# Transformer block: row maxima taken by key blocks ahead of the steps, projections dealt out beside them

## The chip, the cores and the metric

The kernel runs on one core of a Trainium2 chip. The metric is device time in microseconds of one execution, the median of the runs shown; smaller is better. The core's engines are TensorE (PE, with its weight loads PEld), VectorE (DVE), ScalarE (ACT), GpSimd (POOL) and SyncE (SP), which here only issues DMAs. Each engine works through its own queue in order and waits on semaphores for the others.

## The reference, cut to what matters

```python
# x: 1 x 2048 x 576, 32 heads of 18, feed-forward width 4608
qkv = (layernorm(x) @ wqkv)                       # -> q, k, v per head
scores = q @ k.T * 18 ** -0.5
o = softmax(scores) @ v
h = x + o @ wo
g, u = layernorm(h) @ w_gate, layernorm(h) @ w_up
out = h + (gelu_tanh(g) * u) @ w_down
```

Inputs and outputs are float32. The softmax subtracts each row's true maximum, so every score is computed twice: once for the maximum, once for the exponential.

## The kernel before, in words

**Numbers.** Operands are split into two half-precision parts (hi and lo), and a product is a sum of three matmuls, hi·hi, lo·hi, hi·lo. `products` (L264) lists the 14 pairs of one 576-long contraction, `accumulate` (L273) issues them into one PSUM bank.

**Start.** The 2048 rows are cut into 4 blocks of 512. A block is normalized (`ln_stats`, `rstd_of`, `ln_rows`, L372 to L381: DVE, with copies on ACT and differences on POOL), and DMA transposes (`turn`, L230) bring it into XT. The 1152 columns of Q and K are 9 tiles of 128 (tiles 0 to 4 hold Q, 4 to 8 hold K): `qk_tile` (L324) makes one tile for one block, 14 matmuls of 512 columns, ACT takes hi out of the bank, DVE takes lo, and SP stores both to DRAM (L333, L334). `v_rows` (L337) makes V for 128 rows, two times 14 matmuls of 288 columns. An order written out by hand (L404 to L477) interleaves all this; `manual_schedule` keeps PE, ACT, DVE and POOL in program order until L865, and SP in it for L404 to L474. Loads of weights and x are on SP's queue, some placed late in this order. The projections that are left form the generator `other_products` (L785): V of blocks 1 to 3, then Q and K tiles 1, 6, 2, 7, 3, 8 of blocks 1 to 3.

**Attention.** Four heads form a group, 8 groups. For a group, `load_stacks` (L504) reads Q and K from DRAM into a stack set (18 hi, hi, lo rows of each head, two heads to a 128-row tile, so a contraction of 54); half of these loads are on SP, half on POOL. There are two sets, used in turn. A block n (0 to 31) is a group with 512 queries; it has 16 steps, one for each 128 keys.

- *Maxima.* A unit (`max_unit`, L519) is 128 queries against 512 keys for four heads. It has two halves; a half is two matmuls into two banks (L529) and two DVE reductions along them (L532). 16 units make a block. Within a block the query tile t is the slow index, the key block kc the fast one. After 16 units `max_finish` (L540) sends the maxima as two more rows into the Q stacks, so that the score matmul subtracts them. `maxima` (L643) runs through all 512 units, one half per `take`.
- *Scores.* `scores_pair` (L569): two matmuls (L576) into a pair of banks, then one Exp over 1024 columns on ACT (L578) into one of NPE = 4 buffers. Two pairs a step.
- *Weighing.* `weigh` (L580): four matmuls in float32 (L582, eight in the trace) that add the weighted values to `acc`.
- *Block end.* `out_block` (L590) divides by the sums (POOL, and DVE for the last four blocks) and writes into XT.

PSUM has eight banks: two pairs for the scores, one for `acc`, and the three others in a ring for the maxima. Before the steps all four singles are that ring.

**Order of the steps.** After 14 pieces of `other_products`, 24 units (`AHEAD`, L641) run with three pieces after each (L803). Then come 512 steps (L808 to L842). A step issues: half a unit, both score pairs, two pieces of what is left to fill, half a unit, and `weigh` of the step before. The maxima so end 24 steps before the scores. During the last blocks the fill is `wo_block` (L675): the output projection of 128 rows and 288 columns a piece, residual addition on DVE (L684), layer norm, split and transposes, through a single buffer `y`. `prepare_wo` and `split_gate_up` make the next weights ready as `side`.

**Feed-forward.** 9 chunks of 512 columns, gate, up and down (L745 to L782), bound by PE.

## Time and profile before

| what | us |
|---|---|
| three timed runs | 2893.16, 2901.07, 2901.41 |
| median | 2901.07 |
| span of the profiled execution | 2899.4 |
| PE busy in it | 2752.8 |
| DVE busy | 1942.0 |
| ACT busy | 1432.5 |
| POOL busy | 321.8 |

The page gives the span from the first to the last instruction; what lies around it isn't shown by it. Times inside the trace are counted from the span's start. PE counts as busy from the start of a matmul to its modelled end, also where several overlap. In a row of the timeline stand the start, the length, the engine, the line, the operation with what it writes and reads, and the number of instructions merged into it; in square brackets the idle time before it and what ended it. In a row of the chain stand start, length, engine and line. In a row of groups stand after the bar the busy time, the mean length of one in ns, and the idle time before.

### The profile page before, as it was taken

Reading aid. Unit: us, or ns where it says so; the run is one execution under the profiler, and the core shown is the slowest. Engines: PE = TensorE matmul, PEld = TensorE weight load, DVE = VectorE, ACT = ScalarE, POOL = GpSimd, SP = SyncE. Lnnn points to the kernel's source line nnn. Section 1 sums busy time; section 2 is a strip of 40 time slices with the busy share of each in tenths; the row PEclk is TensorE's granted clock in tenths of the full one; section 3 lists DMA queues with packets and bytes.
Section 4 is the critical chain, followed back from the end, with each engine's and each line's share of the span. In section 5 each row is a group of like instructions: output and inputs, shape, how many; then the busy total and the mean of one; then the engine's idle time right before and its main releaser. Section 6 shows DMA issues by size and latency. Waiting matters only on the chain.

```text
span 2899.4 us, 42932 instructions
## 1 busy us (share of the span) xinstructions
PE 2752.8 (95%) x17178; PEld 1152.0 (40%) x17178; DVE 1942.0 (67%) x3485; ACT 1432.5 (49%) x1626; POOL 321.8 (11%) x484
## 2 busy tenths in 40 slices
PE   7999999999999999999887999999999999999999
PEld 3542222222222222222223555555555555555555
DVE  6369999999999999999864725252525252524222
ACT  4217888888888888888563312121212121212111
POOL 2102421222212221212100000000000000000000
PEclk9999999999999999999998999999999999999999
DMA  8211110101001010101113301010101010100001
GB/s 216 67 58 39 40 35 14 38 14 32 14 18 34 14 38 12 35 14 50 40 45 93 96 1 53 1 53 1 53 1 53 1 53 1 53 1 1 1 17 50
DMA packets 109404, 105.08 MB, mean 36 GB/s; under 512 B 61780, under 2 KB 79828, under 8 KB 109204
## 3 DMA queue, kind: packets, MB, share of 16 engines
q1 hardware_dynamic: 102964, 89.98, 11.0%
q0 software_dynamic: 5712, 11.19, 1.4%
q8 instruction: 134, 2.20, 0.3%
q10 hardware_dynamic: 528, 1.18, 0.1%
q14 instruction: 66, 0.54, 0.1%
HBM read 72.09 MB, written 14.42 MB: 30 GB/s over the span
## 4 chain that ended last, share of the span: by engine, by line
PE 50%; DVE 43%; ACT 3%; DMA 2%; issue 1%; SPq 1%; POOL 0%; POOLq 0%; DVEq 0%; ACTq 0%
DVE mx L532 40%; PE pair L278 32%; PE bank L278 16%; PE bank L582 1%; PE bank L529 1%; ACT W L252 1%; ACT V L252 1%; DMA X<-V 0%; ACT V L739 0%; PE pair L576 0%; ACT W L739 0%; DMA X<-A 0%; ACT WK L578 0%; DMA A<-qk_hi 0%; DVE st L185 0%
## 5 line engine op out<-in xcount | busy, mean ns | idle before, releaser
L532 DVE TENSOR_REDUCE mx<-bank 128x1 f32<-128x512 f32 x2048 | 1265.0, 683 | 28.6 <-PE bank L529 28.5
L578 ACT ACTIVATE WK<-pair,p_ex_sc 128x1024 f32<-128x1024 f32 x1024 | 1084.6, 1113 | 235.8 <-PE pair L576 234.8
L582 PE MATMUL bank<-WK,V 128*32 128x512 f32 x4096 | 549.7, 608 | 0.1
L278 PE MATMUL pair<-X,V 128*128 128x512 f16 x2240 | 491.4, 381 | 8.8 <-ACT ga L756 8.6
L278 PE MATMUL pair<-X,W 128*128 128x512 f16 x2044 | 447.4, 379 | 1.5 <-ACT ga L756 1.5
L759 DVE SCALAR_TENSOR_TENSOR ga<-pair,p_hsc,ga 128x512 f32<-128x512 f32 x144 | 107.8, 749 | 506.3 <-PE pair L278 500.6
L278 PEld LDWEIGHTS <-WK 128*128 128x128 f16 x3456 | 338.1, 98 | 93.8 <-issue 0.5
L756 ACT ACTIVATE ga<-pair,p_gsc 128x512 f32<-128x512 f32 x144 | 98.8, 686 | 483.4 <-PE pair L278 483.4
L278 PEld LDWEIGHTS <-W 128*128 128x128 f16 x2296 | 223.7, 98 | 284.5 <-issue 13.6
L529 PE MATMUL bank<-W 54*128 54x512 f16 x1024 | 291.5, 382 | 43.1 <-DVE mx L532 14.1
L278 PEld LDWEIGHTS <-V 128*128 128x128 f16 x2240 | 219.4, 98 | 271.4 <-issue 14.8
L529 PE MATMUL bank<-A 54*128 54x512 f16 x1024 | 279.4, 382 | 36.0 <-DVE mx L532 6.1
L760 ACT CAST WK<-ga 128x512 f16<-128x512 f32 x144 | 88.9, 618 | 436.9 <-DVE ga L759 436.9
L779 DVE SCALAR_TENSOR_TENSOR nat<-bank,p_dsc,nat 128x288 f32<-128x288 f32 x288 | 147.7, 516 | 196.8 <-PE bank L278 196.8
L582 PEld LDWEIGHTS bank<-WK,V 128*32 128x32 f32 x4096 | 81.3, 108 | 434.4 <-issue 406.3
L278 PE MATMUL bank<-V,WK 128*128 128x288 f16 x1920 | 239.5, 286 | 0.2 <-DVE nat L779 0.2
L278 PE MATMUL bank<-W,WK 128*128 128x288 f16 x1536 | 191.4, 286 | 0.0
L576 PE MATMUL pair<-W 56*128 56x512 f16 x1024 | 159.3, 379 | 6.0 <-ACT WK L578 5.4
L576 PE MATMUL pair<-A 56*128 56x512 f16 x1024 | 156.5, 377 | 1.6 <-ACT WK L578 0.8
L761 DVE TENSOR_TENSOR WK<-ga,WK 128x512 f16<-128x512 f32 x144 | 99.3, 690 | 78.1 <-ACT WK L760 77.9
L605 POOL TENSOR_TENSOR rp<-rc,minus_one 128x16 f32<-128x16 f32 x28 | 81.9, 2924 | 616.3 <-DMA rc<-nat 616.3
L529 PEld LDWEIGHTS <-W 54*128 54x128 f16 x1024 | 59.3, 93 | 222.0 <-issue 220.0
(170 smaller groups left out, 1276.9 us busy)
## 6 DMA issues: line engine op xcount, KB each, us to landing
V<-in_B_w_down_dram SPq DMA_DIRECT2D x8, 1152.0 KB
nat<-rc SPq DMA_DIRECT2D x32, 256.0 KB
A<-in_B_w_gate_dram SPq DMA_DIRECT2D x8, 1024.0 KB
A<-in_B_w_up_dram SPq DMA_DIRECT2D x8, 1024.0 KB
qk_hi<-qk SPq DMA_DIRECT2D x36, 128.0 KB
qk_lo<-qk SPq DMA_DIRECT2D x36, 128.0 KB
A<-in_A_x_dram SPq DMA_DIRECT2D x32, 144.0 KB
out_dram<-nat SPq DMA_DIRECT2D x16, 288.0 KB
```

What stands on the lines that cost most here:

```text
L278: nc.tensor.matmul(dst, a, b, start=(i == 0), stop=(i == len(pairs) - 1))
L529: nc.tensor.matmul(pms[j][:, :TB], Q[r, q0 : q0 + P], K[r, kc * TB : (kc + 1) * TB], start=True, stop=True)
L532: nc.vector.tensor_reduce(mx[:, t, 2 * pr + j, kc : kc + 1], pms[j][:, :TB], axis=AX.X, op=ALU.max)
L576: nc.tensor.matmul(pS[:, j, :TB], K[r, kt * P : (kt + 1) * P], Q[r, qc * TB : (qc + 1) * TB], start=True, stop=True)
L578: nc.scalar.activation(pes[(2 * kt + pr) % NPE], pS[:, :, :TB], AF.Exp, scale=ex_sc)
L582: nc.tensor.matmul(acc[32 * hh : 32 * hh + 32, :TB], Vg[n // NB][:, kt * G4 + hh * VC : kt * G4 + hh * VC + 32], pes[(2 * kt + hh // 2) % ...
L605: nc.gpsimd.tensor_tensor(rc, den, minus_one.to_broadcast([P, R]), op=ALU.pow)
L756: nc.scalar.activation(ga, pg[:, :TB], AF.Gelu_apprx_tanh, scale=gsc)
L759: nc.vector.scalar_tensor_tensor(ga, pu[:, :TB], hsc, ga, op0=ALU.mult, op1=ALU.mult)
L760: nc.scalar.copy(hh[:, f], ga)
L761: nc.vector.tensor_sub(hl[:, f], ga, hh[:, f])
L779: nc.vector.scalar_tensor_tensor(nat[:, t, ws], pt[:, :HALF], dsc, nat[:, t, ws], op0=ALU.mult, op1=ALU.add)
```

## The change

The maxima begin earlier, all projections move ahead of the first step, and the maxima that are left are spread evenly over the steps.

1. **Start.** The loads of the K weights and of x for blocks 1 to 3 go on POOL's queue at the very start. Of the hand-written order remain tiles 0, 1, 4, 5, 2, 3, 6, 7 of block 0 and tiles 4, 5 of block 1, with the norms of all four blocks among them. For the first group, the rows of Q and K go from the tile in SBUF straight into the stacks (`stack_rows`, for tiles 0, 4 and 5) and not by way of DRAM. For most tiles the difference lo moves from DVE to a second ACT copy and a POOL subtraction (`pool=True`). V's memsets come later, weights lie in another order in W.
2. **Maxima ahead.** A unit's fast index is now the query tile, the slow one the key block, so that the first units need only key block 0. `accumulate` yields after every five matmuls and says how many columns it issued; `feed` deals out 2300 columns after every half unit until the projections are used up. The units that have run by then (`lead`) are ahead of the steps.
3. **Steps.** One score pair of the next step is issued between the halves. A plan (`wanted`) says how many units should have run after step k; the step takes 0 to 3 halves. NPE is 5. One piece of `fill` a step instead of two.
4. **Output projection.** `y` is a ring of four buffers (two for the last block), and POOL makes the split for blocks 0 to 2.

```diff
+    def feed(it, columns, owed):
+        owed[0] += columns
+        while owed[0] > 0:
+            c = next(it, None)
+            if c is None:
+                return False
+            owed[0] -= c
+        return True
...
+    load_w(wf[1], wqkv[:, D:QK], nc.gpsimd)
+    for b in range(1, NB):
+        load_x(b, nc.gpsimd)
...
+    def stack_rows(j, b, hl):
+        sl = slice(b * TB, (b + 1) * TB)
+        of_k = j > 0
+        first = j * P - (D if of_k else 0)
+        for h in range(4):
+            lo_r, hi_r = max(h * DH, first), min((h + 1) * DH, first + P)
+            if lo_r >= hi_r:
+                continue
+            T = sets[0][h // 2][of_k]
+            o = 64 * (h % 2) + lo_r - h * DH
+            n = hi_r - lo_r
+            src = slice(lo_r - first, hi_r - first)
+            for i, k in enumerate((0, 1, 0) if of_k else (0, 0, 1)):
+                nc.sync.dma_start(T[o + i * DH : o + i * DH + n, sl], hl[src, k])
...
-        nc.vector.scalar_tensor_tensor(lo, bank[:, :TB], 2.0 ** -16, hi,
-                                       op0=ALU.mult, op1=ALU.subtract)
+        if pool:
+            f = next(late_parts)
+            nc.scalar.activation(f, bank[:, :TB], AF.Copy, scale=2.0 ** -16)
+            nc.gpsimd.tensor_sub(lo, f, hi)
+        else:
+            nc.vector.scalar_tensor_tensor(lo, bank[:, :TB], 2.0 ** -16, hi,
+                                           op0=ALU.mult, op1=ALU.subtract)
+        if stack:
+            stack_rows(j, b, hl)
...
+    qk_tiles(0, 4, stack=True)
+    ln_rows(4, 2, **on_pool)
+    qk_tiles(0, 5, stack=True)
+    ln_rows(6, 2, **on_pool)
+    cut(s, 6, 7, 8)
+    qk_tiles(0, 2, 3, pool=True)
+    ln_block(2)
+    ln_rows(8, 4, **on_pool)
+    qk_tiles(0, 6, pool=True)
+    ln_stats(12, 2)
+    qk_tiles(1, 4, stack=True)
+    ln_stats(14, 2)
+    rstd_of(12, TPB, root=True)
+    qk_tiles(1, 5, stack=True)
+    ln_rows(12, 4, **on_pool)
+    qk_tiles(0, 7, pool=True)
...
-        t, kc = divmod(u, NB)
+        kc, t = divmod(u, TPB)
...
-    NPE = 4
+    NPE = 5
...
+    def other_products():
+        for b in (2, 3):
+            for j in (4, 5):
+                yield from qk_tile(j, b, stack=True)
+        yield from qk_tile(0, 1, pool=True, stack=True)
+        for t in range(NT):
+            if t == NT // 2:
+                yield from qk_tile(0, 2, pool=True, stack=True)
+            yield from v_rows(t)
+        yield from qk_tile(0, 3, pool=True, stack=True)
+        for b in range(1, NB):
+            yield from qk_tile(1, b, pool=True)
+        init_set(sets[1])
+        load_stacks(1)
+        yield from qk_tile(8, 0, pool=True)
+        for j in (6, 2, 7, 3, 8):
+            for b in range(1, NB):
+                yield from qk_tile(j, b, pool=True)
+
+    SLACK = 4600
...
+    while more:
+        for _ in range(2):
+            half_units(1)
+            more = feed(fill, SLACK // 2, owed)
...
+    END = NSTEP - NT - 4
+    def wanted(k):
+        loaded = 2 + max(0, (k - 8) // (NB * NT))
+        return min(lead + (NU - lead) * (k + 1) / END, 64 * loaded, NU)
...
+    scores_pair(0, 0, 0)
+    for k in range(NSTEP):
+        n, kt = step(k)
...
+        due = min(3, int(2 * (wanted(k) - state["units"])))
+        scores_pair(n, kt, 1)
+        if due > 1:
+            half_units(1)
+        if k + 1 < NSTEP:
+            scores_pair(*step(k + 1), 0)
+        if k:
+            pn, pk = step(k - 1)
+            weigh(pn, pk, acc)
...
+        take(fill)
+        take(side, 2 if g == NG - 1 else 1)
+        half_units(due - 1 if due > 1 else due)
...
+            y = next(y_pool if b < NB - 1 else y_last)
```

More of the change, by code (lines that the diff above doesn't have):

```diff
@@ new lines, in tile_block @@
+    for t in (2, 3):
+        normed(nat[:, t], nat[:, t], t)
+    take(n0, 3)
+    split_rows(parts[2], nat[:, 2], **on_pool)
+    s = [result(n0), None]
+    idle_products(18)
+    split_rows(parts[3], nat[:, 3])
+    turn(parts[2], 2)
+    turn(parts[3], 3)
+    cut(s, 0, 1, 2, 3, 4)
+    load_w(wf[2], wqkv[:, QK:], nc.sync)
+    take(n1, NK + 1)
+    qk_tiles(0, 0, stack=True)
+    s = [None, result(n1)]
+    cut(s, 4, 5)
+    qk_tiles(0, 1)
+    ln_block(1)
+    qk_tiles(0, 4, stack=True)
@@ L843, in tile_block @@
+        if n and kt in ((3, 6) if late else (2, 4)):
+            take(ob)
+        if late and kt == 9:
+            run(fill)
+            fill = wo_block(qc - 1)
+        if g and g + 1 < NG and kt == 2 and qc == 0:
+            load_stacks(g + 1)
+        if n == NS - NB and kt == 2:
+            load_gate_up(0, nc.gpsimd)
+        if n == NS - 2 and kt == NT * 3 // 4:
+            side = keep(split_gate_up(0, nc.vector.tensor_scalar_mul))
     run(side)
     run(fill)
-    weigh(*prev)
-    ob = out_block(prev[0], prev[2])
+    weigh(*step(NSTEP - 1), acc)
```

260 lines of the change are left out of this document (96 added, 164 removed).

## The prediction, made before the changed kernel had run

> **What bounds the kernel now.** I read the page, then the windows, the groups of the middle stage, one step of the timeline, and the chain of waits. One chip run lies behind all rows: a span of 2899.4 us, 1.7 us under the median of the timed runs (2901.07), and I add that back at the end.
>
> ```profile
> span 2899.4 us, 42932 instructions
> L532 DVE TENSOR_REDUCE mx<-bank x2048: 626/680/693, 120.8 to 1465.1; 128x1 f32<-128x512 f32 x187
> L578 ACT ACTIVATE WK<-pair,p_ex_sc x1024: 1106/1114/1174, 226.4 to 1560.4; 128x1024 f32<-128x1024 f32 x171
> 120.80:226.40 105.60, 102.05 (x592) 49.81 (x593) 72.21 (x117) 19.62 (x46) 0.69 (x3) 0.98 0.16 50
> 226.40:1382.00 1155.60, 1088.29 (x7419) 247.72 (x7418) 1151.00 (x1897) 996.85 (x967) 271.53 (x391) 1.00 0.10 27
> 1382.00:1562.50 180.50, 147.00 (x1016) 54.06 (x1012) 126.34 (x277) 101.78 (x99) 18.81 (x27) 0.91 0.23 56
> L532 DVE TENSOR_REDUCE mx<-bank 128x1 f32<-128x512 f32 x1601 | 988.6, 683 | 0.0
> L578 ACT ACTIVATE WK<-pair,p_ex_sc 128x1024 f32<-128x1024 f32 x800 | 848.4, 1112 | 136.4 <-PE pair L576 135.6
> ```
>
> The first maximum is taken at 120.8, the first Exp at 226.4. In the window rows the columns are length, PE, weight loads, DVE, ACT, POOL. From 120.8 to 226.4 PE is full (102 of 105.6) and DVE is not. From 226.4 to 1382.0 stand 464 of the 512 steps (blocks 0 to 28). The last two rows are groups of 388.2 to 1382.0, 400 steps, so 2.485 us a step: DVE looks full with reductions (988.6 of 993.8), ACT idles 136 us. A step has two half units of maxima (two matmuls and two reductions each), two score pairs with an Exp each, one weigh. So far this says that DVE is the bound. Inside one step it reads otherwise:
>
> ```profile
> 807.46 0.39 PE L529 MATMUL bank<-A 54*128 54x512 f16 x2
> 807.68 0.60 PE L576 MATMUL pair<-W 56*128 56x512 f16 x4
> 808.12 0.88 PE L529 MATMUL bank<-A 54*128 54x512 f16 x2
> 808.63 0.37 PE L529 MATMUL bank<-A 54*128 54x512 f16 x1
> 808.93 1.07 PE L582 MATMUL bank<-WK,V 128*32 128x512 f32 x8
> 809.93 0.39 PE L529 MATMUL bank<-A 54*128 54x512 f16 x2
> 807.88 0.69 DVE L532 TENSOR_REDUCE mx<-bank 128x1 f32<-128x512 f32 x1
> 808.49 1.28 DVE L532 TENSOR_REDUCE mx<-bank 128x1 f32<-128x512 f32 x2
> 810.35 0.69 DVE L532 TENSOR_REDUCE mx<-bank 128x1 f32<-128x512 f32 x1
> 811.09 0.37 PE L529 MATMUL bank<-A 54*128 54x512 f16 x1
> ```
>
> These are PE's issue order (maxima, two score pairs, maxima, weigh, maxima) and single reductions. The second matmul of the second half unit stands alone at 808.63, because its bank, of three, comes free only when the reduction begun at 807.88 ends. From there a **loop** runs: to weigh 0.30 (808.93), weigh to the next maxima 1.00 (809.93), matmul start to reduction start 0.42 (810.35), the reduction 0.69, release 0.05, and at 811.09 the same matmul waits again. That is 2.46, the step. Two reductions in a row take 1.28, so they can start 0.60 apart; four need 2.40 and DVE has a little slack that its busy time hides. PE, the three banks and DVE's latency bound the step together, and PE's order in the queue sets what lies in the loop. The score pairs lie outside it, between the halves.
>
> Without maxima a step is bound by ACT: six Exps in 6.14 are 1.00 apart, so 2.01 a step. PE goes from a score pair to weigh in 0.33.
>
> ```profile
> 1467.99 0.39 PE L576 MATMUL pair<-W 56*128 56x512 f16 x2 [0.54 <-ACT WK L578]
> 1468.32 1.07 PE L582 MATMUL bank<-WK,V 128*32 128x512 f32 x8
> 1492.28 6.14 ACT L578 ACTIVATE WK<-pair,p_ex_sc 128x1024 f32<-128x1024 f32 x6 [2.95 <-PE pair L576]
> ```
>
> **The change, 1: the start.** All projections now end before the first step, so 46 more units run ahead, and the first maximum comes earlier.
>
> ```profile
> 0.00:20.00 20.00, 7.84 (x30) 3.17 (x31) 14.45 (x44) 11.24 (x23) 6.79 (x24) 1.00 0.86 228
> 5.20 6.47 DMA WK<-in_A_wqkv_dram
> 16.48 3.35 DMA X<-A
> 19.96 7.71 PE bank L278 x35
> 15.11 2.74 SPq L231 DMA_TRANSPOSE X<-A  x2
> 1533.28 0.70 SPq L635 DMA_DIRECT2D X<-nat  x1
> 1534.02 0.70 SPq L634 DMA_DIRECT2D X<-nat  x1
> L333 SPq DMA_DIRECT2D qk_hi<-qk x36: 319/320/665, 23.8 to 225.1; - x36
> ```
>
> The last two numbers of the window row are the DMA share, 0.86, and 228 GB/s. The loads of the first weights, landed at 11.7, let projections begin at 19.96. POOL's queue now starts 4.9 MB (the K weights, the x of blocks 1 to 3) beside the first 2.6 MB. At 228/0.86 = 265 GB/s shared evenly, the first 2.6 MB end near 19 instead of 11.7: +7, between 0 (no sharing) and +18 (all of the 4.9 MB first). I take 7, so projections begin near 27. The rule that speaks against this move stands in the Trainium skill, DMA: Bandwidth & Descriptors, Issuing engines are not separate DMA queues: transfers started by different engines end up on the same 16 DMA engines and interleave. By it the even share holds; without it this term would be 0. No row here shows the two queues loading large blocks at once.
>
> Then SP's queue sets the pace. In its fixed order it now issues the stack rows from SBUF to SBUF: 12 for tiles 0 and 4, 3 for tile 5. The nearest row with the same shape (18 rows of 1 KB) is issued every 0.74 (1533.28 to 1534.02). Ahead of block 1's last transpose stand 27 x 0.74 = 20.0, eight stores of 0.32 = 2.6, four transposes of 1.37 = 5.5, in all 28 from 31.5 (tile 0 done), and 3.4 to land: 63. PE then owes tiles (4, block 1), (5, block 1) and 7, 9 us, and DVE closes block 3's norm: first maximum near **76**, against 120.8 (60, if a stack row costs SP only the 0.32 of a store and the weights come on time; 90, if they come last). Behind it SP still has 4 + 4 transposes and the stacks of blocks 1 to 3; key block 2 lands near 101 where the maxima want it at 96, key block 3 some 2.5 late too: **8** us (0 to 15). Hi and lo conversions, now by ACT and POOL for most tiles, hide under PE, which needs 3 us a tile; the V memsets hide on POOL.
>
> ```profile
> 148.53 2.68 PE pair L278 x21
> 191.80 4.64 PE pair L278 x21
> 1416.71 0.32 PE bank L529 x2
> 1413.17 3.54 PE bank L278 x28
> 1418.78 3.54 PE bank L278 x28
> ```
>
> From the first maximum to the first step PE does 26 tiles of 14 matmuls at 4.64/21 = 0.221, 80.4; 448 V matmuls at 2.68/21 = 0.128, 57.2; and, one half unit per 2300 columns, 315392/2300 + a few = 140 halves at 0.32 between wide matmuls, 44.8. Sum 182; DVE needs 140 x 1.20 and some 8 for splits, 176, and hides beside it. So the lead is 70 units, and steps start at 76 + 182 + 8 = **266** (245 to 285): **+40** on 226.4.
>
> **2: the steps.** PE's order is now: score pair 1, maxima, score pair 0 of the next step, weigh, maxima. The three banks stay. With two halves the lonely second matmul is that of the first half, and between it and the next maxima stand a score pair (0.22, from 807.46 to 807.68) and weigh: 0.22 + 0.33 + 1.00 + 0.42 + 0.69 + 0.05 = **2.70** instead of 2.46. Queued behind the waiting matmul are that score pair, weigh and so the next maxima; DVE waits for these, 0.3 a step. The second score pair hides in the reduction. A step with one half has no matmul that waits: two pairs, 0.33 and weigh, **1.76** from maxima to maxima; ACT's 2.01 is met on the average with its longer neighbours, thanks to the fifth buffer.
>
> Up to step 464 the plan asks for 0.898 units a step, 833 halves. It is capped at 128 units until step 72: eight steps with none (2.01), then about twelve with three (2.70 + 1.20). The other 444 have 798 halves: 354 with two, 90 with one. 354 x 2.70 + 90 x 1.76 + 8 x 2.01 + 12 x 3.90 = 955.8 + 158.4 + 16.1 + 46.8 = 1177. The reduction at a block's end fits into DVE's idle time.
>
> ```profile
> 403.37 0.50 POOL L517 DMA_DIRECT2D A<-qk_hi  x1 [0.55 <-DMA A<-qk_lo]
> A<-qk_hi POOLq DMA_DIRECT2D x32, 72.0 KB, 6.7
> ```
>
> Step 72 wants the stacks of the next heads 16 us after block 4 begins. Now their last is issued 15 us after it (403.4 against 388.2) and lands 6.7 later, behind POOL's reciprocal work: 5 us of wait, and 1 at step 136. So 1183, 2.55 a step, against 1155.6: **+27** (an average of 2.40 a step would give -42, 2.65 gives +74).
>
> **3: the end.** Blocks 29 to 31 now take one piece of the output projection a step instead of two, POOL splits three row blocks, and four y buffers replace one. Before, such a step lasted 5.6 (1413.17 to 1418.78), and 12 us went into two waits:
>
> ```profile
> PE bank L131 <- DVE am_gu L127: 7.6, 1, 7.6
> DVE WK L214 <- POOL V L228: 4.5, 2, 2.3
> ```
>
> PE stood before the exponents' transposes, DVE before POOL had read y (us in total, times, longest). After, a step with one product is 2.70 + 1.8 + about 0.5 for DVE's addition in its line, 5.0; without maxima 3.4. Block 29: 10 x 2.5 + 6 x 5.0 = 55; block 30: 56; block 31: 48 with 4 of waiting for the last rows; 3.4 left over: 162 against 180.5: **-18** (-30 to 0). What follows 1562.5 is unchanged.
>
> **The sum:** +40 + 27 - 18 = +49 on the span, and 2901 + 49 = **2950**.
>
> **The rivals.**
> - *DVE is the bound (faster).* Its occupancy speaks for it, the 0.60 spacing against it. A half would cost 2.485/2 = 1.24 wherever it stands: 833 x 1.24 + 16 of idle + 6 = 1055, -100 instead of +27: 2901 - 78 = 2823. It decides if the loop breaks, which needs a fourth bank or a shorter queue. The Trainium skill, Perfetto Trace Analysis, Identifying the Most-Contended Engine, takes the occupancy of the vector engine as a fair measure of its distance from the roofline; by that rule this rival would be the forecast, while the row at 808.63 speaks against it.
> - *The order costs nothing.* Steps with two halves stay at 2.485, those with one fall to ACT's 2.01: 354 x 2.485 + 90 x 2.01 + 16 + 12 x 3.7 + 6 = 1127, -29: 2901 + 40 - 29 - 18 = 2894, no change. For it: the loop's extra 0.24 is a sum of gaps, each taken from another order.
> - *A step with one half lasts as long as ACT, 2.01, and the first maxima wait for SP until 86 (slower still):* 90 x 0.25 + 10 = +32: 2982.
> - That the maxima don't run 70 ahead is ruled out by the count of columns above.
>
> **How the numbers follow.** Forecast 0.52, DVE bound 0.15, order free 0.17, slower still 0.16. The predicted time is the forecast's. 0.3% (9 us) is about what a measurement of this kernel tells from no change. Faster by more: 0.15, and 0.08 of the second rival and of the forecast's low edge: 0.23. Within: 0.11. Slower: 0.66. The likeliest case has 2905 to 2995 for itself: its terms' ends lie some 20, 55 and 15 away, the root of their squares is 60, and three quarters of it are taken; the range reaches down over the second rival, 2865, and up to 2995, and leaves out DVE bound and the worst of the last.
>
> **What would show it.** Right: the first reduction near 76 and the first Exp near 266; steps of about 2.70 and 1.76 in the middle with DVE idle some 0.3 before a reduction that waits for PE; a stretch of 2.0 then 3.9 near step 64. Wrong: an average step under 2.4, single second matmuls that don't wait, or a first Exp before 240.

## The result, and the profile after

The changed kernel takes **2995.21 us** (median of 4 runs, 2993.31 to 3000.92) against 2901.24 of the kernel before (4 runs beside it): ratio **1.034**, 95% interval 1.0322 to 1.0357. The direction was forecast; the size was about half of what came, and 2995.21 lies just above the range's top of 2995. The profiled execution of the changed kernel is the longest of its four, 3000.92 (5.7 above the median), and its span is 2999.1; so some 6 of the 51 in the last row below belong to that execution.

Cut at the same marks as in the prediction (step 464 is the first of block 29; "last Exp" is the start of the last one), the spans are:

| stretch, us | before | forecast | after | missed by |
|---|---|---|---|---|
| start to the first reduction of the maxima | 120.8 | 76 | 83.8 | +8 |
| first reduction to first Exp | 105.6 | 190 | 202.8 | +13 |
| steps 0 to 463 | 1155.6 | 1183 | 1186.8 | +4 |
| step 464 to the last Exp | 178.3 | 160 | 172.2 | +12 |
| last Exp to the end | 1339.0 | 1339 | 1353.4 | +14 |
| span | 2899.4 | 2948 | 2999.1 | +51 |

So the middle, on which most of the prediction's argument stood, came out within 4, and the two ends were sized wrong, all in one direction.

From the page of the changed kernel, the groups of the reductions and of the Exps (line numbers have moved: reduction L542, its matmuls L539, score matmuls L586, Exp L588, weigh L592, accumulate L277), and below them the reductions in the page of the kernel before:

```profile
span 2999.1 us, 43163 instructions
...
L542 DVE TENSOR_REDUCE mx<-bank 128x1 f32<-128x512 f32 x2048 | 1277.6, 683 | 161.6 <-PE bank L539 159.1
L588 ACT ACTIVATE WK<-pair,p_ex_sc 128x1024 f32<-128x1024 f32 x1024 | 1105.2, 1116 | 242.3 <-PE pair L586 231.7
```

```profile
L532 DVE TENSOR_REDUCE mx<-bank 128x1 f32<-128x512 f32 x2048 | 1265.0, 683 | 28.6 <-PE bank L529 28.5
```

DVE now idles 161.6 ahead of its reductions, where it was 28.6, and PE ends that idling. The windows of the changed kernel for the three middle stretches follow, the last one up to the end of the last Exp. The columns are as in the prediction; the third number from the right is PE's granted clock as a share of full speed.

```profile
83.80:286.60 202.80, 193.67 (x1084) 81.47 (x1084) 183.09 (x299) 52.17 (x123) 42.34 (x69) 0.99 0.24 69
286.60:1473.40 1186.80, 1047.70 (x7220) 236.08 (x7223) 1041.23 (x1700) 1013.51 (x956) 261.05 (x367) 0.99 0.09 23
1473.40:1647.10 173.70, 143.15 (x990) 49.30 (x983) 122.91 (x247) 104.35 (x100) 28.64 (x36) 0.94 0.24 55
```

In the steps no engine is full any more: DVE is busy for 1041 of 1187, where it was 1151 of 1156. One step with two halves, from the timeline of the changed kernel:

```profile
1007.96 0.37 PE L539 MATMUL bank<-A 54*128 54x512 f16 x1 [0.34 <-DVE mx L542]
1007.96 0.59 PE L586 MATMUL pair<-A 56*128 56x512 f16 x2
1008.48 1.07 PE L592 MATMUL bank<-WK,V 128*32 128x512 f32 x8
1009.48 0.39 PE L539 MATMUL bank<-A 54*128 54x512 f16 x2
1009.70 0.38 PE L586 MATMUL pair<-A 56*128 56x512 f16 x2
1009.92 0.38 PE L539 MATMUL bank<-A 54*128 54x512 f16 x1
1010.65 0.37 PE L539 MATMUL bank<-A 54*128 54x512 f16 x1 [0.34 <-DVE mx L542]
1009.90 2.48 DVE L542 TENSOR_REDUCE mx<-bank 128x1 f32<-128x512 f32 x4 [0.20 <-PE bank L539]
```

The single matmul at 1007.96 waits for a bank. Behind it go the score pair and weigh (1008.48, +0.52), the next maxima (1009.48, +1.00), their first reduction (1009.90, +0.42), and when that ends the same matmul of the next step (1010.65, +0.75). The period is 2.69; 2.70 was forecast.

### The profile page after: what moved, and what is told of

Same layout as the page of the kernel before. It is cut to its first block, busy times and chain, and to the rows that moved or that the text cites. A ratio compares the mean times of both kernels' runs of the same rounds, so it can differ in the third digit from the quotient of the medians.

```text
span 2999.1 us, 43163 instructions
## 1 busy us (share of the span) xinstructions
PE 2758.4 (92%) x17178; PEld 1139.6 (38%) x17178; DVE 1932.1 (64%) x3434; ACT 1468.8 (49%) x1652; POOL 368.6 (12%) x525
## 4 chain that ended last, share of the span: by engine, by line
PE 78%; DVE 12%; ACT 3%; DMA 2%; issue 2%; POOL 1%; SPq 1%; POOLq 0%; ACTq 0%; DVEq 0%
PE pair L277 32%; PE bank L592 16%; PE bank L277 15%; PE bank L539 11%; DVE mx L542 10%; PE pair L586 4%; ACT V L252 1%; ACT W L252 1%; DMA X<-V 1%; DMA A<-qk_hi 0%; ACT V L751 0%; ACT W L751 0%; SPq L372 0%; DMA V<-in_B_w_down_dram 0%; DMA nat<-rc 0%
## 5 line engine op out<-in xcount | busy, mean ns | idle before, releaser
L542 DVE TENSOR_REDUCE mx<-bank 128x1 f32<-128x512 f32 x2048 | 1277.6, 683 | 161.6 <-PE bank L539 159.1
L588 ACT ACTIVATE WK<-pair,p_ex_sc 128x1024 f32<-128x1024 f32 x1024 | 1105.2, 1116 | 242.3 <-PE pair L586 231.7
L592 PE MATMUL bank<-WK,V 128*32 128x512 f32 x4096 | 554.1, 613 | 0.1
L277 PE MATMUL pair<-X,W 128*128 128x512 f16 x2296 | 518.1, 382 | 15.4 <-DMA qk_hi<-qk 7.6
L277 PE MATMUL pair<-X,V 128*128 128x512 f16 x2240 | 491.2, 380 | 18.4 <-ACT ga L768 18.4
L277 PEld LDWEIGHTS <-WK 128*128 128x128 f16 x3456 | 338.2, 98 | 93.7 <-issue 0.5
L539 PE MATMUL bank<-W 54*128 54x512 f16 x1024 | 280.6, 384 | 81.3 <-DVE mx L542 79.3
L539 PE MATMUL bank<-A 54*128 54x512 f16 x1024 | 267.4, 387 | 73.2 <-DVE mx L542 66.8
L277 PEld LDWEIGHTS <-W 128*128 128x128 f16 x2296 | 219.4, 98 | 288.8 <-issue 41.2
L277 PEld LDWEIGHTS <-V 128*128 128x128 f16 x2240 | 219.2, 98 | 280.5 <-issue 23.8
L277 PE MATMUL bank<-V,WK 128*128 128x288 f16 x1920 | 239.1, 286 | 0.3 <-DVE nat L791 0.3
L586 PE MATMUL pair<-W 56*128 56x512 f16 x1024 | 230.6, 385 | 4.3 <-ACT WK L588 4.2
L586 PE MATMUL pair<-A 56*128 56x512 f16 x1024 | 230.2, 381 | 2.7 <-ACT WK L588 2.0
L277 PE MATMUL bank<-W,WK 128*128 128x288 f16 x1536 | 191.4, 286 | 0.0
L592 PEld LDWEIGHTS bank<-WK,V 128*32 128x32 f32 x4096 | 81.2, 108 | 208.4 <-issue 205.2
L539 PEld LDWEIGHTS <-W 54*128 54x128 f16 x1024 | 57.0, 94 | 260.6 <-issue 240.6
L539 PEld LDWEIGHTS <-A 54*128 54x128 f16 x1024 | 55.2, 94 | 252.6 <-issue 237.9
L773 DVE TENSOR_TENSOR WK<-ga,WK 128x512 f16<-128x512 f32 x144 | 99.4, 690 | 78.1 <-ACT WK L772 78.0
```

The lines of the kernel that those rows point to most:

```text
L277: nc.tensor.matmul(dst, a, b, start=(i == 0), stop=(i == n - 1))
L539: nc.tensor.matmul(pms[j][:, :TB], Q[r, q0 : q0 + P], K[r, kc * TB : (kc + 1) * TB], start=True, stop=True)
L542: nc.vector.tensor_reduce(mx[:, t, 2 * pr + j, kc : kc + 1], pms[j][:, :TB], axis=AX.X, op=ALU.max)
L586: nc.tensor.matmul(pS[:, j, :TB], K[r, kt * P : (kt + 1) * P], Q[r, qc * TB : (qc + 1) * TB], start=True, stop=True)
L588: nc.scalar.activation(pes[(2 * (n * NT + kt) + pr) % NPE], pS[:, :, :TB], AF.Exp, scale=ex_sc)
L592: nc.tensor.matmul(acc[32 * hh : 32 * hh + 32, :TB], Vg[n // NB][:, kt * G4 + hh * VC : kt * G4 + hh * VC + 32], pes[(2 * (n * NT + kt) + ...
```

## The experiments

The stretches of all runs, from their traces. Seven runs are alike up to the first maxima (after, e1, e2, e8, e3, e5, e12) and put the first reduction at 83.5 to 87.0, so some 3 us of it belong to the run. Times with an interval are medians of at least 4 runs; three are single runs. The kernel before ran again beside each set of experiments, with medians from 2894.9 to 2901.2, so that times of different sets compare to some 0.2%.

| run | first reduction | first Exp | steps 0 to 463 | 464 to last Exp | after it | time | ratio to before (95%) |
|---|---|---|---|---|---|---|---|
| before | 120.8 | 226.4 | 1155.6 | 178.3 | 1339.0 | 2901.24 | 1 |
| after | 83.8 | 286.6 | 1186.8 | 172.2 | 1353.4 | 2995.21 | 1.034 (1.0322–1.0357) |
| e1_order | 87.0 | 289.8 | 1129.5 | 166.1 | 1351.9 | 2938.53 | 1.0145 (1.0128–1.0162) |
| e2_no_spread | 84.2 | 285.8 | 1251.1 | 154.2 | 1353.2 | 3046.14 | single run |
| e8_half_reduce | 84.3 | 285.7 | 1090.7 | 167.5 | 1354.6 | 2900.38 | single run |
| e16_before_half | 120.6 | 227.0 | 1042.6 | 173.0 | 1339.1 | 2783.46 | single run |
| e7_part4 | 119.9 | 225.4 | 1154.8 | 165.8 | 1341.0 | 2888.83 | 0.9975 (0.9963–0.9987) |
| e3_burst | 86.4 | 290.4 | 1190.8 | 169.8 | 1353.3 | 2996.09 | 1.0355 (1.0333–1.0377) |
| e4_loads | 87.4 | 291.5 | 1187.1 | 170.2 | 1354.1 | 3003.23 | 1.037 (1.0355–1.0386) |
| e5_tail | 83.5 | 286.3 | 1189.3 | 168.6 | 1347.2 | 2992.3 | 1.0333 (1.0316–1.035) |
| e6_all | 87.2 | 290.5 | 1128.7 | 165.1 | 1341.8 | 2930.06 | 1.0119 (1.0104–1.0134) |
| e9_loads_behind | 79.5 | 283.4 | 1187.8 | 170.4 | 1352.7 | 2993.25 | 1.0333 (1.0318–1.0349) |
| e10_two_queues | 72.1 | 274.8 | 1183.5 | 169.3 | 1353.0 | 2985.64 | 1.0313 (1.0294–1.0333) |
| e12_half_lead | 85.3 | 270.3 | 1138.3 | 165.6 | 1351.0 | 2927.18 | 1.0107 (1.0092–1.0122) |
| e13_all | 72.6 | 275.2 | 1131.2 | 167.0 | 1342.9 | 2914.16 | 1.0063 (1.0048–1.0078) |
| e14_norm_behind | 72.6 | 275.3 | 1185.2 | 169.6 | 1353.1 | 2986.02 | 1.0302 (1.0287–1.0318) |
| e15_all_half_lead | 72.7 | 252.2 | 1138.2 | 166.4 | 1342.6 | 2902.18 | 1.0014 (1.0004–1.0023) |

### The steps: order, spread, and the length of a reduction

**e1_order** puts PE's order of before into the changed steps:

```diff
-    scores_pair(0, 0, 0)
     for k in range(NSTEP):
...
-        scores_pair(n, kt, 1)
         if due > 1:
             half_units(1)
-        if k + 1 < NSTEP:
-            scores_pair(*step(k + 1), 0)
-        if k:
-            weigh(...)
+        scores_pair(n, kt, 0)
+        scores_pair(n, kt, 1)
         take(fill)
         take(side, 2 if g == NG - 1 else 1)
         half_units(due - 1 if due > 1 else due)
+        if k:
+            weigh(...)
```

> The changed kernel with PE's order inside a step as it was before the change (a half unit of maxima, both score pairs of this step, the other half unit, weigh); the plan that spreads the maxima, the 70 units of lead, the start and the end stay. Loop theory (PE's order, the three banks and the reductions' latency bound the step): a step with two halves goes from 2.70 back to 2.46, one with one half stays at ACT's 2.01 or under, so steps 0 to 463 last 354 x 2.46 + 90 x 2.01 + 8 x 2.01 + 12 x 3.6 = 1111 to 1135 instead of 1187, and the time is 2995 - 52 to - 76, 2920 to 2943. Rival (DVE's occupancy is the bound, a half costs 1.25 of DVE wherever it stands): the order changes nothing, 1187 and 2995. Rival (ACT's Exp is the bound and waits for nothing but its own pace): no change either.

Measured: 1129.5 for the steps, 2938.53. The order alone is worth 57. Where it sits is one row of PE's waits during steps 0 to 463, first of the changed kernel, then of e1 (total, times, longest):

```profile
PE bank L539 <- DVE mx L542: 128.1, 369, 0.9
```

```profile
PE bank L539 <- DVE mx L542: 10.6, 38, 1.4
```

PE waited 369 times for a bank; the plan has 354 steps with two halves and 12 with three. In the old order nearly all of these waits are gone. Both rivals (DVE or ACT as the bound, the order without effect) fall.

**e2_no_spread** gives every step its two halves until the units run out:

```diff
-        return min(lead + (NU - lead) * (k + 1) / END, 64 * loaded, NU)
+        return min(lead + k + 1, 64 * loaded, NU)
...
-        due = min(3, int(2 * (wanted(k) - state["units"])))
+        due = min(2, int(2 * (wanted(k) - state["units"])))
```

> The changed kernel without the spread: two halves in every step until all units are done (never one, never three), in the changed order of PE; the lead, the start and the end stay. The 442 units left after the lead then end at step 442 instead of being thinned out to step 492. Loop theory: nearly every step up to 464 costs 2.70, so the stretch lasts 434 x 2.70 + 22 x 2.01 + 8 = 1224, 37 more than the 1187 of the changed kernel, and the late blocks get a little shorter because they hold no maxima (28 steps x 0.3 = 8 less at least). Occupancy rival: about the same number of halves done a little earlier, 51 halves more by 1.25 = 64 more up to step 464, and the same 64 less behind it. What tells them apart is the period of a step with two halves in the middle: 2.70 (loop) against 2.50 (occupancy), and DVE's idle time ahead of a reduction.

Measured: blocks that hold two halves in every step last 2.69 a step, as the loop says (2.50 was the occupancy's number). The stretch came to 1251 where I had 1224, the late steps gave 18 back: so in this order the spread was worth 45 to 50 (spans of 3044.3 and 2999.1; 3046 in one run against the median of 2995). The sum of 1224 counts only 434 + 22 of the 464 steps, and the eight that it leaves out, at 2.70, are 22 of the 27.

**e8_half_reduce** and **e16_before_half** shorten the reduction, in the changed kernel and in the kernel before:

```diff
-                nc.vector.tensor_reduce(..., pms[j][:, :TB],
+                nc.vector.tensor_reduce(..., pms[j][:, : TB // 2],
```

> The changed kernel with each reduction of the maxima over 256 of the 512 keys (half of the keys are left out of the maxima; matmuls, banks and order stay). A reduction should last 0.69 - 256 x 0.00104 = 0.42. Loop theory: only one reduction stands in the loop, so a step with two halves goes from 2.70 to 2.43 and steps 0 to 463 from 1187 to about 1090 (354 x 0.27 less); ACT idles still. Occupancy rival: DVE's work in a step with two halves falls from 2.5 to 1.4, below ACT's 2.01, so that all steps go to ACT's pace: 464 x 2.01 = 933, with 10 to 20 more for what is around.

> The kernel before with each reduction of the maxima over 256 of the 512 keys (half of the keys are left out of the maxima; everything else stays). It asks the prediction's first claim of the kernel before itself. Loop theory (score pair, weigh, the next maxima, one reduction and the release of a bank follow each other): one reduction stands in the loop, a step of two halves goes from 2.485 to 2.485 - 0.265 = 2.22, and steps 0 to 463 from 1155.6 to 1030 to 1045. Rival (DVE was the bound there: in the trace of before it waited for PE only 1.0 in the 1155.6): DVE's work per step falls to 1.4, and the steps go to ACT's pace of 2.01: 933 to 955.

Measured, in a single run each: 1090.7 and 1042.6. Both stand where the loop put them (1090; 1030 to 1045) and far from the occupancy (933 to 955). The timeline of e8 shows DVE's two bursts of a pair of steps, one with two halves and one with one:

```profile
805.91 1.42 DVE L542 TENSOR_REDUCE mx<-bank 128x1 f32<-128x256 f32 x4 [1.00 <-PE bank L539]
808.33 0.76 DVE L542 TENSOR_REDUCE mx<-bank 128x1 f32<-128x256 f32 x2 [1.00 <-PE bank L539]
810.11 1.42 DVE L542 TENSOR_REDUCE mx<-bank 128x1 f32<-128x256 f32 x4 [1.02 <-PE bank L539]
```

The pair lasts 4.20, and 2.43 + 1.76 = 4.19 was forecast: one reduction is in the loop, not four. In e16 16 of the 29 blocks last 2.23 a step (forecast 2.22) and most of the others up to 2.27, with DVE's work in the steps cut by 39%:

```profile
227.00:1269.60 1042.60, 1001.38 (x7417) 223.61 (x7415) 706.37 (x1896) 992.05 (x967) 270.77 (x391) 1.00 0.11 30
```

DVE fell from 1151 to 706, the stretch from 1156 to 1043.

### The output projection alone

**e7_part4** is the kernel before with only the changed `wo_block`:

```diff
-    y = view(WK, 2 * 4 * TB * NPE, (D,))
+    y_pool = ring([view(V, GU + 4 * D * i, (D,)) for i in range(4)])
+    y_last = ring([view(WK, 2 * FT * TB * 4 + 4 * D * i, (D,)) for i in range(2)])
...
+            y = next(y_pool if b < NB - 1 else y_last)
             normed(y, nat[:, t], t)
-            if b == 0:
+            if b < NB - 1:
                 split_rows(ys[t % 2], y, nc.gpsimd.tensor_copy, nc.gpsimd.tensor_sub)
```

> The kernel before with only the changed output projection: four y buffers for blocks 0 to 2 and two for the last, and POOL splits the rows of blocks 0 to 2 instead of block 0 alone; start, lead, steps and the two pieces a step stay as before. My theory: the two waits of the late blocks before (7.6 of PE ahead of the exponents, 4.5 of DVE behind POOL's reading of y) shrink, 5 to 12 less: ratio 0.996 to 0.998. Rival: POOL's y split (three passes of a row instead of DVE's) stands ahead of its work for the next attention block and delays the transposed rows, as the changed kernel's trace shows it at 1606 to 1609: 0 to 8 slower, ratio 1.000 to 1.003.

Measured: ratio 0.9975 (7.7 less than the kernel before beside it), the late stretch 12.5 shorter, the tail 2.0 longer. This part of the change pays by itself, and it makes **the fastest version of the study**. Of the waits named, the exponents' one (L131) fell from 7.6 to 2.4. The longest wait of PE that is left is the one for rows of XT (L278), 6.8, which was 9.4:

```profile
PE bank L278 <- DMA X<-nat: 6.8, 2, 5.7
...
PE bank L131 <- DVE am_gu L127: 2.4, 1, 2.4
```

The wait of DVE for POOL's reading of y is gone from the list.

### The start and the tail

**e3_burst** doubles the bursts ahead of the steps:

```diff
-        for _ in range(2):
-            half_units(1)
-            more = feed(fill, SLACK // 2, owed)
+        half_units(2)
+        more = feed(fill, SLACK, owed)
```

> The changed kernel with the maxima ahead of the steps dealt out by whole units (four maxima matmuls, then 4600 columns of projections) instead of half units (two, then 2300). My theory: each change between maxima and projections costs PE about 0.11 beyond the work itself; half as many changes, 70 x 2 x 0.11 = 15 less between the first reduction (83.8) and the first Exp (286.6), which comes at 272; the time falls to 2980. Rival: the extra time of that stretch is the projections' own (waits for the tiles' banks and stores), and the change does nothing, or waits on the three banks grow with the longer bursts: 286 to 292 and 2995 to 3000.

Measured: 204.0 from first reduction to first Exp against 202.8, and 2996.09; no gain. My theory falls as it was put. The changed kernel's timeline shows where the forecast's 0.32 for a half was too low:

```profile
105.17 0.39 PE L539 MATMUL bank<-A 54*128 54x512 f16 x2
105.49 1.25 PE L277 MATMUL pair<-X,W 128*128 128x512 f16 x5
106.67 0.39 PE L539 MATMUL bank<-A 54*128 54x512 f16 x2
107.00 1.04 PE L277 MATMUL pair<-X,W 128*128 128x512 f16 x4
107.97 0.39 PE L539 MATMUL bank<-A 54*128 54x512 f16 x2
```

A half with five wide matmuls takes 1.50, with four 1.30; less 0.221 each, 0.40 and 0.42 are the half's. That is 140 x 0.09 = 12.6, the missing 13. It agrees with the whole stretch: 202.8 less the forecast's 80.4 and 57.2 of projections and less 9.1 in which PE is idle leaves 56.1, 0.40 for each of the 140 halves. In whole units every second burst meets the three banks, as e3's timeline shows:

```profile
151.86 0.60 PE L539 MATMUL bank<-A 54*128 54x512 f16 x4
152.39 1.89 PE L277 MATMUL pair<-W,X 128*128 128x288 f16 x14
154.22 0.97 PE L539 MATMUL bank<-A 54*128 54x512 f16 x4
155.12 2.50 PE L277 MATMUL pair<-W,X 128*128 128x288 f16 x19
```

From its start to the projections behind it a unit takes 0.53 or 0.90, so that what fewer changes save is partly given back; and this run's granted clock in the stretch was 0.97 instead of 0.99. How much is left of the gain at equal clock isn't settled.

**e4_loads** moves POOL's loads behind POOL's split of row 2:

```diff
-    load_w(wf[1], wqkv[:, D:QK], nc.gpsimd)
-    for b in range(1, NB):
-        load_x(b, nc.gpsimd)
...
     split_rows(parts[2], nat[:, 2], **on_pool)
+    load_w(wf[1], wqkv[:, D:QK], nc.gpsimd)
+    for b in range(1, NB):
+        load_x(b, nc.gpsimd)
```

> The changed kernel with POOL's loads of the K weights and of x for blocks 1 to 3 issued after POOL's split of row 2 instead of at the start. My theory: they no longer share the DMA engines with the first weights; these land at about 12 instead of 25.1, the first projection starts at 20 to 21 instead of 32.7, and the queue of SP, which is full from the first tile's stack rows on, moves with it: first reduction at 71 to 74 instead of 83.8, first Exp 10 to 13 earlier, the time 2983 to 2985. Rival: what arrives last at the first maximum is not SP's queue but the x of blocks 1 to 3, which then land later: first reduction at 84 or later and no gain.

A miss. In the changed kernel ACT takes the five chunks of the first weights as they land (the first and the last):

```profile
14.41 0.68 ACT L152 ACTIVATE A<-WK 128x576 f16<-128x576 f32 x1 [5.51 <-DMA WK<-in_A_wqkv_dram]
...
25.12 0.68 ACT L152 ACTIVATE A<-WK 128x576 f16<-128x576 f32 x1 [1.95 <-DMA WK<-in_A_wqkv_dram]
```

In e4 the last is taken at 11.59, and yet PE begins no earlier:

```profile
34.65 5.56 PE L277 MATMUL pair<-X,W 128*128 128x512 f16 x14 [17.96 <-issue]
```

```profile
20.00:30.00 10.00, 0.00 (x0) 0.00 (x0) 0.00 (x0) 3.44 (x10) 0.00 (x0) 0.50 1.04 340
```

At 18.7 DVE and ACT had nothing left to do for this tile; what it still lacked were transposed rows, and the DMA engines were full (1.04, 340 GB/s) with the loads issued at 15 to 19: from 20 to 30 POOL's queue moved 3.24 MB and SP's, with the transposes, 0.15 MB. The rival's number held, but not its cause, the late x. **e9_loads_behind** tests the transposes: a copy on POOL reads the transposed rows ahead of the loads.

```diff
     cut(s, 0, 1, 2, 3, 4)
-    load_w(wf[2], wqkv[:, QK:], nc.sync)
+    nc.gpsimd.tensor_copy(landed, XT[:, 0, 0:TB:P])
+    load_w(wf[1], wqkv[:, D:QK], nc.gpsimd)
+    for b in range(1, NB):
+        load_x(b, nc.gpsimd)
+    load_w(wf[2], wqkv[:, QK:], nc.gpsimd)
```

> The changed kernel with POOL's loads (K weights, x of blocks 1 to 3, now also the V weights) issued behind a small copy on POOL that reads a column of each of block 0's four transposed row blocks, so that they start only when these have landed. The experiment with the loads behind row 2's split brought nothing: the first weights came early, but the first projection still began at 34.65, in a stretch with the DMA engines full. Theory: there the transposes of rows 2 and 3 landed late, among 4.6 MB of loads issued just ahead of them; with the loads behind the landing, the first projection begins at 20 to 21, SP's queue (full from 36.6 on in the changed kernel) begins 11 earlier, the first reduction comes at 72 to 75, the time is 2983 to 2987. Rival: something else holds the first projection until 33, or block 1's x, now later, becomes what comes last: first reduction at 82 or later, 2995 to 3005.

```profile
19.89 3.18 PE L277 MATMUL pair<-X,W 128*128 128x512 f16 x14 [2.93 <-issue]
...
31.07 11.37 PE L277 MATMUL pair<-X,W 128*128 128x512 f16 x42
```

The first tile begins 13 earlier than in the changed kernel (32.71), as forecast, and 15 earlier than in e4, so late transposes were e4's cause. Of these 13 only 4 reach the first reduction (79.5, not 72 to 75), and the time is 2993.25 (2983 to 2987 was forecast): the next tile waits until 31. In the changed kernel SP is full from the first tile's stack rows on, and in e9 these begin at 31.07 instead of 36.55:

```profile
36.55 9.16 SPq L372 DMA_DIRECT2D A<-qk  x12
45.76 0.47 SPq L393 DMA_DIRECT2D qk_hi<-qk  x1
...
47.77 9.04 SPq L372 DMA_DIRECT2D A<-qk  x12
```

```profile
27.13 0.68 ACT L152 ACTIVATE A<-WK 128x576 f16<-128x576 f32 x1 [9.28 <-DMA WK<-in_A_wqkv_dram]
...
30.47 0.57 ACT L379 ACTIVATE qk<-pair 128x512 f16<-128x512 f32 x1
```

The second fence is ACT in e9: tile 0's conversion (30.47) stands in ACT's queue behind the norm of the K weights, and that waits for their load. **e10_two_queues** takes a third of the stack rows off SP, **e14_norm_behind** then moves the norm behind tile 0:

```diff
+                eng = nc.gpsimd if i == 2 else nc.sync
-                nc.sync.dma_start(T[...], hl[src, k])
+                eng.dma_start(T[...], hl[src, k])
```

```diff
-    take(n1, NK + 1)
     qk_tiles(0, 0, stack=True)
+    take(n1, NK + 1)
```

> The same, and the third copy of each stack row goes by POOL's queue instead of SP's, so that 18 instead of 27 of these transfers stand on SP ahead of block 1's last transpose. If SP's queue paces the first maximum (0.75 a row), the first reduction comes 9 x 0.75 = 7 earlier than with the loads alone, at 65 to 68, and key blocks 2 and 3 come earlier too: 2975 to 2980. Rival: the norm of block 1 or the tiles' own conversions come last: no change against the loads alone.

> The loads behind the landing and two queues for the stack rows, and the K weights' norm moved behind tile 0 on ACT. With the two edits alone the first tile is done at 22.8, but ACT converts it only at 30.2, behind the norm's five squares, which wait for the K weights until 26.9; SP's first stack row goes out at 30.8. Theory: SP's queue now starts some 7 earlier, at 23.5 to 24, and its eight rows and stores for tile 0 are done before tile 4 arrives; but tile 4's conversion waits for the norm, which starts no earlier, so that the first reduction gains only what SP issued ahead, 3 to 6 of the 7: first reduction at 66 to 69, time 2980 to 2984. Rival: the K weights set the first maximum (their norm, split and tiles 4 and 5 follow at 26.9 whatever SP does): first reduction stays at 72, time 2985.

Nine rows fewer brought 7.4 (79.5 to 72.1; 7 was forecast), so SP's queue is on the path there. The first reduction itself was forecast at 65 to 68 and the time at 2975 to 2980, from an e9 that came 4 to 7 later than expected. e14 starts SP's rows at 23.26 instead of 30.81, and gains nothing:

```profile
23.26 6.10 SPq L369 DMA_DIRECT2D A<-qk  x8
...
42.00 6.33 SPq L369 DMA_DIRECT2D A<-qk  x8
```

Its rival holds: tile 4's rows go out at 42.00 as in e10 (42.05), since the K weights' arrival (27), norm, split and tiles 1 and 4 lie ahead of them.

**e5_tail** takes two pieces of the output projection a step again:

```diff
-        take(fill)
+        take(fill, 2)
         take(side, 2 if g == NG - 1 else 1)
```

> The changed kernel with two pieces of the output projection a step in the late blocks, as before the change, instead of one. My theory of the tail: the stretch from the last Exp to the end is 14 longer because products of block 30's output projection are left over behind the last step, and their row split on POOL stands ahead of the weights' load for the down product and of the transposes. With two pieces a step nothing is left over: the tail goes from 1353 to 1339 to 1343, the late steps grow by up to 5 from three products left to do inside them, the time 2983 to 2990. Rival: POOL's split and the y buffers cost the tail whatever is left over: no change.

Behind the last Exp, the changed kernel's PE and ACT:

```profile
1646.45 5.32 PE L277 MATMUL bank<-W,X 128*128 128x288 f16 x42
...
1673.21 20.77 PE L277 MATMUL pair<-X,V 128*128 128x512 f16 x84 [14.30 <-ACT ga L768]
```

```profile
1671.18 1.28 ACT L768 ACT_TABLE_LOAD   x1 [17.72 <-DMA X<-V]
```

Three products (42 matmuls) are left over ahead of the last weigh; then the norm, POOL's split and the transposes follow each other, and ACT's queue stands before its load of the down weights, which go where the split rows still are. Before, that wait was 10.23 and PE's 6.79. Behind the last Exp PE is now idle for 26.0 (1353.5 less 1327.45 busy) and was for 16.1 (1339.0 less 1322.87); its busy time grew by 4.6, as long as the leftover products last. e5 shortens the tail by 6.2 and the late steps by 3.6, less than forecast (a tail of 1339 to 1343, a time of 2983 to 2990): its time only falls to 2992.3. With the old step order the tail falls by 10 (e1 to **e6_all**, which also has e3 and e4: 1351.9 to 1341.8). Why it gives less in the new order is open.

**e6_all** is the edits of e1, e3, e4 and e5 together, **e13_all** those of e1, e5, e9 and e10:

> The changed kernel with the step's order of before, whole units in the bursts ahead, POOL's first loads later, and two pieces a step in the late blocks (the four edits of the other experiments together). If the four costs are separate they add up: 2995 - 57 - 15 - 11 - 10 = 2902, ratio 1.002 to the kernel before, with the steps at 1130, the first Exp at 262 and the tail near 1341. If the start's two edits share one cover (SP's queue), 2910 to 2920.

> The step's order of before, two pieces a step in the late blocks, and the start of the two experiments above (loads behind the landing, two queues for the stack rows). If these terms add up: 2930 of the run with all earlier edits, less 12 for the loads and 7 for the queue, 2911 (2905 to 2918), ratio 1.003 to 1.008 to the kernel before. If the start has another limit: 2925 to 2932.

e6 came to 2930.06, a miss: order and pieces add up (2938.5 less 8.5), the two edits at the start give nothing, as they did alone. e13 came to 2914.16, as forecast.

### Does a lead pay at all

**e12_half_lead** is e1 with half the maxima ahead, **e15_all_half_lead** is e13 with that and e14's norm:

```diff
-    SLACK = 4600
+    SLACK = 9200
```

> The changed kernel with the step's order of before and half the lead: one half unit of maxima per 4600 columns of projections, so about 36 units instead of 70 run ahead. Theory: a unit ahead costs the start about as much as it saves in the steps, because PE is full in both: 34 units less are 68 halves by 0.40 (55.4 over 138 in the profile of the changed kernel) = 27 less before the first Exp, and some 64 of the steps up to 464 get two halves instead of one, 64 x (2.46 - 2.01) = 29 more. Time 2934 to 2945, first Exp near 263, steps 0 to 463 near 1158. Rival: the maxima ahead hide beside the projections: first Exp stays at 287 to 290 and the time is 2965.

> All edits that helped, together, with half the lead: the step's order of before, two pieces a step in the late blocks, loads behind the landing, two queues, the norm behind tile 0, one half unit per 4600 columns. Theory: the time of the run with all of them and the full lead (2914.16) less the 11 that half the lead gave alone and less what the norm gives: 2897 to 2904, ratio 1.000 to 1.003 to the kernel before; so the maxima ahead, in the best form tried, just break even, and the output projection's part alone (2888.83) stays the fastest. Rival: half the lead gains nothing once the start is quicker, because PE then waits for x: 2910 to 2916.

e12 is faster than its expectation, 2927.18. The start gave only 18 of 27, because PE now reached the last key block's rows before they had landed, and then ran at a lower granted clock (0.61 from 99.4 to 103.2; 3.75 for ten matmuls that take 2.32 otherwise):

```profile
99.42 3.75 PE L277 MATMUL pair<-X,W 128*128 128x512 f16 x10 [9.19 <-DMA X<-V]
```

But the steps rose by 9 only, where I had 29. With 70 units ahead the plan meets the cap of two groups (128 units) at step 64, the first of block 4: in e1 blocks 4, 5 and 8 last 3.43, 2.58 and 2.78 a step beside 2.38 of their neighbours, 26.5 us in all, with a wait for the stacks of up to 7.2; with 36 ahead these blocks last 2.45, 2.45 and 2.45. A larger lead so runs into the stacks. Every run with 70 ahead has such a wait of PE near step 72, of 4.4 to 7.2, with a lower granted clock behind it (0.50 from 467.9 to 472.6 in e1); e12 and e15 have neither. e15, the best form of the idea tried, comes to 2902.18, ratio 1.0014: against the profile of before +26 at the first Exp, -17 in the steps, -12 late, +4 after. The -12 late is what e7 has by itself (-12.5), and e7 stands at 0.9975: the rest of the change, in its best form tried, still costs some 0.4%.

## Why the prediction was right or wrong

**What bounds the kernel (right).** The loop through PE's order, three banks and one reduction was read from the kernel before, and e16 bears it out there (2.228 against 2.22) as e8 does after. The busy times of before alone did not decide it: ahead of its reductions DVE waited for PE only 1.0 in all of steps 0 to 463. The Trainium skill, Perfetto Trace Analysis, Identifying the Most-Contended Engine, takes the vector engine's occupancy as a measure of how near the bound is; with 1151.00 of 1155.60 busy it pointed to DVE, and the rival built on that (2823) fell.

**Steps (right, +27 forecast, +31 measured).** 2.70 for two halves (2.69), 12 steps with three after a stretch at the cap (blocks 4 and 5: 3.61 and 2.81 a step), a wait for the next stacks (5 + 1 forecast, 6.3 measured). "The order costs nothing" fell by e1. One cost was not in the sum: behind PE's wait of 6.28 for the stacks its granted clock was 0.50, and four steps with three halves lasted 5.39, 5.39, 5.38 and 4.97 instead of 3.88, about 6 in all. The first row below is that stretch, the second one like it soon after:

```profile
475.09:491.25 16.16, 15.05 (x58) 2.02 (x58) 10.60 (x19) 6.69 (x7) 0.48 (x3) 0.50 0.06 13
496.21:515.63 19.42, 15.64 (x94) 3.30 (x90) 18.40 (x31) 11.62 (x11) 0.00 (x0) 1.00 0.01 1
```

So the 4 by which the steps were missed are smaller than this one term, and the other steps came out some 2 under their sum.

**Start (wrong in size, +40 forecast, +60 measured).** Two terms failed. *"The first 2.6 MB end near 19 instead of 11.7"*: they were taken at 25.1, inside the stated bounds of 0 and +18 but well off the even share. POOL's loads and SP's do interleave on the same DMA engines, as the Trainium skill states in DMA: Bandwidth & Descriptors, Issuing engines are not separate DMA queues; the trace agrees (25.1 with POOL's loads beside them, 11.59 in e4 without), and e4 adds that the transposes share them too (34.65 against 19.89 in e9). What failed is "shared evenly", which that section does not state of the bytes. From 8 to 14 and from 14 to 20 of the changed kernel the queues (q0 is POOL's, q1 is SP's) moved, in packets, MB and share of the 16 DMA engines:

```profile
q0 software_dynamic: 319, 1.25, 65.8%
q1 hardware_dynamic: 319, 0.65, 37.6%
q0 software_dynamic: 345, 1.52, 70.1%
q1 hardware_dynamic: 343, 0.69, 34.8%
```

The packets were shared evenly, but POOL's were twice as large, so SP's loads got a third of the bytes. The assumed 265 GB/s was not the limit: 334 were moved from 5 to 25. So tile 0 was done 5 later than forecast (SP's rows begin at 36.55, not 31.5), SP's queue then took 30.8 up to block 1's last transpose where 28 was forecast, and the first reduction came 8 later. *"140 halves at 0.32 between wide matmuls, 44.8"*: a half costs 0.40 to 0.42 there. The price was the length of one row at 1416.71, and not the distance that a half puts between the projections on its two sides. The waits of 8 forecast beside it were right in sum (9 of idle PE), though by luck: DVE's reductions caused 7.6 of them, not the stacks.

**End (wrong).** *"-18 (-30 to 0)"* was -6: PE waited 11.7 for rows of XT where 4 were allowed, and blocks 30 and 31 took 61.6 and 60.7 instead of 56 and 48, while block 29 took 49.9 instead of 55. *"What follows 1562.5 is unchanged"* failed outright, +14: the prediction counted 3.4 left over for PE and did not follow these products through DVE, POOL, the transposes and the buffer up to ACT's queue. e5 and e6 show 6 to 10 of it as the price of one piece a step; the other 4 or so, which also e7 (+2), e13 and e15 (+4) have in part, come with POOL's slower split, which is argued from the trace and not shown, since it was not tried by itself.

**Range.** Two terms lay beyond their own ends: the first Exp at 286.6 (245 to 285), and the tail, which had no term and no end at all and added 14. Three quarters of the root of the squares lets errors cancel; here all five stretches came out longer than forecast. That the sum passed the top by 0.2 only is chance; the terms of the start and the tail were wrong by themselves.

## What to carry to other kernels

A row at 99% busy names a suspect, and the test is cheap: halve its work and see whether the time follows. Follow a loop of waits through engines and buffers, and price a change of order by what enters that loop. Work that is run ahead has to find a stretch with a free engine; here PE was full in the start as well, so a unit ahead cost there at least what it saved later (from 70 to 36 ahead the start became 18 shorter and the steps 9 longer), and beyond the next group's operands it only waited.

## What the runs showed of the hardware that was not expected

- **Two queues on the same DMA engines:** where POOL's and SP's loads ran together (8 to 20 of the changed kernel), each moved about as many packets (319 and 319, 345 and 343), and the one with the larger packets twice the bytes. In e4, from 20 to 30, 768 packets of POOL's moved 3.24 MB beside 631 of SP's with 0.15 MB, and the first tile began 15 later than in e9, where the transposes went ahead of the loads. One queue alone reached the same rate: SP's 339 GB/s at a DMA share of 0.98 (e4, 5 to 10), against 340 at 1.04 there.
- **SBUF to SBUF by 18 rows:** SP issues one in 0.75 to 0.76 (12 in 9.16), about twice its 0.3 to 0.5 for the store of a whole tile; nine fewer moved the first reduction by 7.4.
- **PE behind a long wait:** the first tile took 5.56 in e4 after 18 us without work, at a granted clock of 0.56, and 3.18 in e9 after 2.9, at 1.00. In the steps of the changed kernel 6.28 us of waiting were followed by 16 us at 0.50, so that the wait cost about twice its length.
